# A linear-attention and two-MoE kernel: the first slot's transposes behind the last attention product, the last routing step earlier, slot 1's transposes inside layer 2, the next weights behind its rows

## The chip, the cores and the metric

The kernel runs on one core of a Trainium2 chip. The metric is the device time of one execution in microseconds (us), from the first to the last instruction of the core and what the program needs around it. A core has five engines with instruction queues of their own: TensorE (PE: matrix products and transposes; weight loads are listed as PEld), VectorE (DVE), ScalarE (ACT), GpSimd (POOL) and SyncE (SP, which here only issues DMAs). They meet through semaphores. POOL issues the indirect DMAs (gathers and scatters by row number), SP the plain ones.

## The reference

Three stages follow each other. The first is a linear attention with decay over 4 batches, 8 heads, 768 positions of 64 numbers in blocks of 64. Its output, 3072 rows of 512 numbers, goes through two mixtures of experts with 8 experts each, in which every row takes the one expert that its router prefers:

```python
for b in range(nb):                                   # attention, block by block
    intra = (qb @ kb.T * Dmask) @ vb
    inter = (qb * lam_pow) @ kv_state
    out[:, :, sl] = intra + inter
    kv_state = lam_block * kv_state + (kb * rev_pow).T @ vb
x = attn_out.transpose(0, 2, 1, 3).reshape(B * S, H * D)
...
logits = x @ w_gate + modality_bias[modality_id]      # first MoE
e_idx = np.argmax(logits, axis=1)                     # gate_w: softmax at e_idx
for e in range(E):
    h = np.maximum(x[mask] @ w1[e], 0.0)              # 512 -> 1024
    out[mask] = gate_w[mask, None] * (h @ w2[e])      # 1024 -> 512
...
do_compute = x @ w_skip > 0                           # second MoE: only these rows
y[mask] = gate_w[mask, None] * (h @ w2[e]);  out[do_compute] = xc + y
```

## The kernel before

**Attention.** 24 units (6 chunks of 128 positions times 4 batches) run through a pipeline written out by hand. In step i of the loop `for i in range(N + 1)`, PE makes unit i-1's product with the state (`stage_inter`), unit i's state update (`stage_kv`), unit i-1's product within the block (`stage_intra`; with the first it is the attention output, which ACT copies into `xr`), unit i+1's transposes and scores, and `stage_x(i - 2)`: four transposes of a finished `xr` into the bank `pmi`, from which ACT copies them to `xt` for the router. The routing of a chunk of four units is cut into `route_1` (router product from `xt`), `route_2` and `route_3` (choice of the expert, on DVE), `route_4` (ranks within the expert, two small products on PE, and the gate on DVE) and `route_5` (four indirect writes by POOL into a table in DRAM, `tab`, that lists each expert's rows). The last chunk's routing is done within the first slot of the MoE.

**Slots.** A MoE works through slots of 256 rows of one expert. A slot reads its list of rows (`load_ix`, SP), gathers the rows (`gather_x`, POOL, two halves of 128 rows), transposes them (`trans_x`: per half four transposes on PE, a cast `xth` by ACT, the remainder `xtl = x - xth` by DVE), and runs `layer1` and `layer2`. Every operand is split into a rounded high part and a low part, so each product is three matmuls (high x high, high x low, low x high). `layer1` is 8 steps f of 12 matmuls of 256 columns; after every second step ACT writes `hh` (relu) and DVE `hl` (its low part). `layer2` runs once for each half j of the rows: 8 steps of 3 matmuls of 512 columns, two steps for each quarter g of the weights `w2h[g]`, `w2l[g]`. Weights arrive in `raw1` and `raw2`; `split_w1` and `split_w2` cast the high part on ACT (L294, L300) and subtract on DVE (L295, L301).

**Order.** All instructions of an engine stay in the order in which the program calls them. In `layer1(kk, steps)` the entry `steps[f]` is called right behind the instructions of step f, so it decides what DVE, ACT and PE do between two steps. `table(which)` is a generator of three parts on DVE: the first ends with the first rows of all slots, which `load_ix` needs; the second says which expert comes next, which `ld_w1` and `ld_w2` need; the third says which slots are more than half full.

The first slot of the first MoE is `first1()`: it takes the largest expert on the rows counted so far, so its weights and rows are loaded during attention. In the last steps of attention its w1 is split in halves by the table `SPL`. `trans_x(0, 0, ...)` writes the attention's bank pair `psS`; here the second half's transposes carry a wait for DVE's `xtl` of the first half. The first slot of the second MoE is `first2()`, whose body `arm` is built the same way; in it `split_w2` and `layer2` take the quarters in the order 3, 2, 1, 0, and `ld_w1` there waits for the gathered rows (a dependency "the rows first"). The remaining slots are unrolled with runtime branches (`slots`, `slot`).

## Time and profile before

| | |
|---|---|
| median of 3 runs | 757.86 us (755.03 to 761.19) |
| the profiled execution | 751.07 us, its span 749.4 us |
| PE busy | 674.8 us, 90% of the span |
| DVE, ACT, POOL busy | 357.6, 266.6, 251.0 us |
| mean granted TensorE clock | 0.962 of full speed |

The span falls into attention (to about 137 us), the first MoE (to about 500 us) and the second (to the end). PE is busy throughout the middle of both MoEs, and its idle stretches lie at the seams: at the end of attention, in the first slot and at the first slot of the second MoE. A busy share says little of such a seam; the rows below show who waits for whom in these places. Times in them are microseconds from the start of the span; in brackets stands how long the engine was idle before, and what ended that.

### The profile page before, as it was taken

To read this page: it belongs to the slowest core of one execution; us is meant where nothing else is said; L and a number is where in the kernel's file an instruction comes from. 1 tells how busy PE (TensorE), PEld (TensorE's weight loads), DVE (VectorE), ACT (ScalarE), POOL (GpSimd) and SP (SyncE) were. 2 spreads that over 40 slices of the span, in tenths; PEclk is the share of its full clock that TensorE was granted. 3 is DMA by queue.
4 is the path that set the end of the run, shared out by engine and by line. 5 is a ranking of instruction groups with operands and counts; after the bars stand their busy time and mean duration, and the time that the engine had idled before them with its cause. 6 is when DMAs were issued, how large, how long until landed. Compare 5 with 4: busy or idle time off the path is not lost. (4 is left out here: it accounts for less than half of the span.)

```text
span 749.4 us, 18996 instructions
## 1 busy us (share of the span) xinstructions
PE 674.8 (90%) x7060; PEld 593.2 (79%) x7060; DVE 357.6 (48%) x873; ACT 266.6 (36%) x472; POOL 251.0 (33%) x306
## 2 busy tenths in 40 slices
PE   6878787769999999979999998877899999998994
PEld 5667666658889888778899887766799998897993
DVE  5455465481233025661331335646424566576850
ACT  2444242432222214642222225343013455546540
POOL 6445354343222224463122313461311221122231
PEclk9999899698999999989999999899899999999998
DMA  9757579219122212884111211450631766757600
GB/s 298 233 180 225 164 208 302 64 31 337 59 72 97 86 48 70 291 289 141 69 59 63 67 49 42 141 197 5 212 125 53 248 213 211 235 197 228 219 19 27
DMA packets 56568, 110.04 MB, mean 147 GB/s; under 512 B 18272, under 2 KB 18400, under 8 KB 56400
## 3 DMA queue, kind: packets, MB, share of 16 engines
q1 hardware_dynamic: 44432, 86.65, 35.6%
q0 software_dynamic: 9744, 20.47, 8.3%
q8 instruction: 76, 1.25, 0.7%
q10 hardware_dynamic: 2224, 0.93, 0.5%
q14 instruction: 92, 0.75, 0.4%
HBM read 84.08 MB, written 30.06 MB: 152 GB/s over the span
## 5 line engine op out<-in xcount | busy, mean ns | idle before, releaser
L716 PE MATMUL p<-xth,w1h 128*128 128x256 f32 x672 | 194.6, 290 | 10.1 <-DVE nm L151 4.5
L718 PE MATMUL p<-xth,w1l 128*128 128x256 f32 x672 | 189.2, 281 | 0.1
L717 PE MATMUL p<-xtl,w1h 128*128 128x256 f32 x672 | 189.2, 282 | 0.0
L724 DVE SCALAR_TENSOR_TENSOR hl<-p,hh 128x512 fp32r<-128x512 f32 x84 | 57.9, 691 | 190.2 <-ACT hh L723 190.2
L759 PE MATMUL p<-w2h,hl 128*128 128x512 f32 x360 | 143.3, 398 | 4.1 <-DVE hl L724 4.1
L716 PEld LDWEIGHTS p<-xth,w1h 128*128 128x128 f32 x672 | 128.8, 192 | 21.0 <-issue 12.9
L757 PE MATMUL p<-w2h,hh 128*128 128x512 f32 x360 | 143.6, 399 | 0.7 <-ACT hh L723 0.7
L758 PE MATMUL p<-w2l,hh 128*128 128x512 f32 x360 | 142.6, 396 | 1.3 <-DVE w2l L301 1.3
L161 POOL DMA_INDIRECT out_dram<-x2r,it x43 | 50.0, 1162 | 244.1 <-DVE x2r L768 114.9
L717 PEld LDWEIGHTS p<-xtl,w1h 128*128 128x128 f32 x672 | 129.2, 192 | 0.7
L718 PEld LDWEIGHTS p<-xth,w1l 128*128 128x128 f32 x672 | 128.8, 192 | 0.3 <-DVE w1l L625 0.3
L723 ACT ACTIVATE hh<-p 128x512 fp32r<-128x512 f32 x84 | 50.3, 598 | 195.4 <-PE p L718 187.8
L759 PEld LDWEIGHTS p<-w2h,hl 128*128 128x128 f32 x360 | 68.6, 190 | 18.8 <-DVE hl L724 4.8
L758 PEld LDWEIGHTS p<-w2l,hh 128*128 128x128 f32 x360 | 68.6, 190 | 16.7 <-DVE w2l L301 1.9
L757 PEld LDWEIGHTS p<-w2h,hh 128*128 128x128 f32 x360 | 68.6, 191 | 15.2 <-ACT hh L723 0.9
L165 POOL DMA_INDIRECT xg<-xs,it x54 | 62.0, 1147 | 40.9 <-issue 17.9
L161 POOL DMA_INDIRECT tab<-pk,rows x28 | 29.7, 1060 | 100.3 <-issue 85.6
L765 ACT ACTIVATE x2r<-p,it 128x512 f32<-128x512 f32 x26 | 17.9, 689 | 114.1 <-PE p L759 102.3
L300 ACT CAST w2h<-raw 128x1024 fp32r<-128x1024 f32 x48 | 48.8, 1049 | 25.7 <-issue 14.7
L301 DVE TENSOR_TENSOR w2l<-raw,w2h 128x1024 fp32r<-128x1024 f32 x45 | 52.3, 1220 | 9.1 <-ACT w2h L300 8.6
L295 DVE TENSOR_TENSOR w1l<-raw,w1h 128x1024 fp32r<-128x1024 f32 x38 | 51.7, 1419 | 2.4 <-ACT w1h L294 1.9
L473 POOL TENSOR_TENSOR qs<-kq,ltab 128x512 f32<-128x512 f32 x24 | 30.5, 1272 | 39.2 <-PE psO L534 28.7
(211 smaller groups left out, 867.3 us busy)
## 6 DMA issues: line engine op xcount, KB each, us to landing
raw<-in_w_dram SPq DMA_DIRECT2D x96, 512.0 KB, 6.8
kq<-in_qkv_dram SPq DMA_DIRECT2D x24, 512.0 KB, 5.5
xs<-x2r SPq DMA_DIRECT2D x28, 256.0 KB, 2.0
v<-in_qkv_dram SPq DMA_DIRECT2D x24, 256.0 KB, 4.1
xs<-xr SPq DMA_DIRECT2D x24, 256.0 KB, 4.6
xs<-xgm SPq DMA_DIRECT2D x7, 512.0 KB, 4.6
xg<-xs,it POOLq DMA_INDIRECT x54, 4.4
tab<-tini ACTq DMA_DIRECT2D x2, 416.0 KB, 7.5
```

Source lines behind the costliest of these rows:

```text
L161: nc.gpsimd.indirect_dma_start(out=dst, out_offset=bass.IndirectOffsetOnAxis(ap=idx, axis=0), in_=rows, in_offset=None, bounds_check=dst.s ...
L165: return nc.gpsimd.indirect_dma_start(out=rows, out_offset=None, in_=src, in_offset=bass.IndirectOffsetOnAxis(ap=idx, axis=0), bounds_chec ...
L295: (nc.gpsimd if c in pool else nc.vector).tensor_tensor(out=w1l[c], in0=raw1[:, c], in1=f32(w1h[c]), op=ALU.subtract)
L301: (nc.gpsimd if c in pool else nc.vector).tensor_tensor(out=w2l[c], in0=r, in1=f32(w2h[c]), op=ALU.subtract)
L716: nc.tensor.matmul(o, w1h[c][:, fs], xh[:, c, :], start=(c == 0), stop=False)
L717: nc.tensor.matmul(o, w1h[c][:, fs], xl[:, c, :], start=False, stop=False)
L718: nc.tensor.matmul(o, w1l[c][:, fs], xh[:, c, :], start=False, stop=(c == 3))
L723: nc.scalar.activation(out=a, in_=pt, func=AF.Relu)
L724: nc.vector.scalar_tensor_tensor(out=b, in0=pt, scalar=0.0, in1=f32(a), op0=ALU.max, op1=ALU.subtract)
L757: nc.tensor.matmul(p2[j], a, w2h[g][:, i], start=(n == 0), stop=False)
L758: nc.tensor.matmul(p2[j], a, w2l[g][:, i], start=False, stop=False)
L759: nc.tensor.matmul(p2[j], b, w2h[g][:, i], start=False, stop=(n == 7))
```

## The change

Five edits:

- `trans_x(0, 0, ...)` moves from ahead of the last `stage_intra` to behind the attention loop, and `stage_x(N - 1)`, until now step 0 of the first `layer1`, follows it there. The last quarter of w1 is split one attention step earlier (`SPL`).
- In the first `layer1` the last chunk's routing is called one step earlier (`route_1` in step 0 in place of 1, `mid` in 1 in place of 2, `late` in 3 in place of 4). The four splits of w2 are spread over steps 2, 3, 6 and 7, and the first part of the table moves from `late` to step 5.
- `layer2` gets a call `mid` behind its sixth step (18 of 24 matmuls). Slot 1's `trans_x` goes there, into the second half of slot 0's `layer2`; it stood ahead of that half. The conditional split of w1 (`split_next`) goes behind that half.
- `ld_w1` of the next expert in `first1` waits until both halves of slot 1's rows have landed (`behind`); on SP `ld_w2` and later DMAs are queued behind it.
- In `arm` the quarters of w2 are split and used in the order 0, 1, 2, 3.

```diff
-        SPL = {22: ((0, 0),), 23: ((0, 1), (0, 2)), 24: ((0, 3),)}
+        SPL = {22: ((0, 0),), 23: ((0, 1), (0, 2), (0, 3))}
...
-            if i == N:
-                trans_x(0, 0, [psS[:, j].rearrange("p (a t) -> p a t", t=P) for j in range(2)])
             if i:
                 stage_intra(i - 1)
...
         assert not sc
+        trans_x(0, 0, [psS[:, j].rearrange("p (a t) -> p a t", t=P) for j in range(2)])
+        stage_x(N - 1)
...
-    def layer2(which, kk, j, order=range(4)):
+    def layer2(which, kk, j, mid=None):
...
             nc.tensor.matmul(p2[j], b, w2h[g][:, i], start=False, stop=(n == 7))
+            if n == 5 and mid:
+                mid()
...
+    def behind(first, got):
+        for g in got:
+            tc.add_manual_dep(first.ins, g.ins.name, mybir.DependencyInfo(mybir.DependencyClass.Sync, mybir.DependencyReason.DATA),
+                              reason="the rows first")
...
                 route_5(NC - 1, t)
-            next(tb)
-            split_w2([0, 1])
+            split_w2([1])
...
-        layer1(0, {0: lambda: stage_x(NC * B - 1), 1: route_1, 2: mid, 4: late, 6: lambda: split_w2([2, 3])})
+        layer1(0, {0: route_1, 1: mid, 2: lambda: split_w2([0]), 3: late, 5: lambda: next(tb), 6: lambda: split_w2([2]),
+                   7: lambda: split_w2([3])})
...
+        got = gather_x(0, 1)
         e = reg(0, 2, 0, NE - 1)
-        ld_w1(e)
+        behind(ld_w1(e), got)
         ld_w2(e)
-        for i in range(1, 3):
-            gather_x(0, i)
+        gather_x(0, 2)
         fill()
         layer2(0, 0, 0)
-        trans_x(0, 1, ptr)
         fl = flag(0, 1)
+        layer2(0, 0, 1, lambda: trans_x(0, 1, ptr))
         split_next(0, 1, fl)
-        layer2(0, 0, 1)
...
-            split_w2([3, 2])
-            l1(0, {0: la, 1: lambda: (lg(), rk()), 3: lambda: rb(pcnt[1]), 5: lambda: (next(tb), split_w2([1, 0]))})
+            split_w2([0, 1])
+            l1(0, {0: la, 1: lambda: (lg(), rk()), 3: lambda: rb(pcnt[1]), 5: lambda: (next(tb), split_w2([2, 3]))})
...
-            layer2(1, 0, 0, (3, 2, 1, 0))
+            layer2(1, 0, 0)
```

The end of attention on PE. L534 is `stage_inter`, L545 `stage_intra` (`v` and the scores `P` into `psO`), L357 `stage_x`, L335 `trans_x` (`xg_157` and `xg_158` are the two halves of slot 0's rows); + and - are after and before.

```order
 L534 MATMUL psO<-s_2730,qs 64x64
+L545 MATMUL psO<-v,P 64x64 x16
+L357 MATMUL pmi<-ident,xr_189 128x128 x4
 L335 MATMUL psS<-ident,xg_157 128x128 x4
 L335 MATMUL psS<-ident,xg_158 128x128 x4
-L545 MATMUL psO<-v,P 64x64 x16
-L357 MATMUL pmi<-ident,xr_189 128x128 x4
```

The last product of attention and unit 22's transposes come ahead of slot 0's transposes.

DVE in the first `layer1`, between `route_3` (L133, the running counts `rs`) and `route_4` (L141, L143): L301 makes a low quarter of w2, L724 `hl`.

```order
 L133 TENSOR_TENSOR rs_123<-rs_123,oh 128x8 x4
-L724 SCALAR_TENSOR_TENSOR hl_2858<-p_2873,hh_2856 128x512
+L301 TENSOR_TENSOR w2l_153<-raw_140,w2h_149 128x1024
+L724 SCALAR_TENSOR_TENSOR hl_2863<-p_2878,hh_2861 128x512
 L141 COPY rs_123<-rs_123 128x8
 L143 TENSOR_TENSOR rk<-oh,pmi 128x32
```

The first quarter of w2 is now split ahead of `route_4` on DVE.

PE at slot 1's transposes (L335 into `ptr`, from `xg_159` and `xg_160`) within slot 0's `layer2` (L757 to L759; `w2h_149` to `w2h_152` are the quarters 0 to 3). Before:

```order
L759 MATMUL p_2875<-w2h_152,hl_2859 128x512
L335 MATMUL ptr_2871<-ident,xg_159 128x128 x4
L335 MATMUL ptr_2872<-ident,xg_160 128x128 x4
L757 MATMUL p_2876<-w2h_149,hh_2856 128x512
L758 MATMUL p_2876<-w2l_153,hh_2856 128x512
```

After:

```order
L759 MATMUL p_2881<-w2h_151,hl_2864 128x512
L335 MATMUL ptr_2876<-ident,xg_159 128x128 x4
L335 MATMUL ptr_2877<-ident,xg_160 128x128 x4
L757 MATMUL p_2881<-w2h_152,hh_2862 128x512
L758 MATMUL p_2881<-w2l_156,hh_2862 128x512
```

The 18 matmuls of the first three quarters of the second half now stand ahead of the transposes, the 6 of the last quarter behind them.

PE at the start of `layer2` in `arm`, the first slot of the second MoE (`hh1`, `hl1` are the second half of the hidden rows, `hh0`, `hl0` the first). Before:

```order
L718 MATMUL p10_2870<-xth0_167,w1l3_148 128x256
L757 MATMUL p20_2875<-w2h3_152,hh1_2857 128x512
L758 MATMUL p20_2875<-w2l3_156,hh1_2857 128x512
L759 MATMUL p20_2875<-w2h3_152,hl1_2859 128x512
L757 MATMUL p20_2875<-w2h3_152,hh1_2857 128x512
```

After:

```order
L718 MATMUL p10_2875<-xth0_167,w1l3_148 128x256
L757 MATMUL p20_2880<-w2h0_149,hh0_2861 128x512
L758 MATMUL p20_2880<-w2l0_153,hh0_2861 128x512
L759 MATMUL p20_2880<-w2h0_149,hl0_2863 128x512
L757 MATMUL p20_2880<-w2h0_149,hh0_2861 128x512
```

The quarter that needs the last written part of `hl` comes last in place of first.

## Rows read from the trace of the kernel before

**Rows 1.** Timeline of PE, end of attention (start us, us, engine, line, operation, count)

```profile
129.82 0.37 PE L545 MATMUL psO<-v,P 64*64 64x64 f32 x2
...
136.66 1.11 PE L335 MATMUL psS<-ident,xg 128*128 128x128 f32 x4 [1.83 <-DMA xg<-xs,it]
139.17 1.12 PE L335 MATMUL psS<-ident,xg 128*128 128x128 f32 x4 [1.40 <-DVE xtl L339]
140.22 1.14 PE L545 MATMUL psO<-v,P 64*64 64x64 f32 x32
...
142.10 0.58 PE L716 MATMUL p<-xth,w1h 128*128 128x256 f32 x1
```

**Rows 2.** Timeline of ACT, the splits of w1 in the last attention steps

```profile
129.47 1.14 ACT L624 CAST w1h<-raw 128x512 fp32r<-128x512 f32 x2
...
134.28 2.18 ACT L624 CAST w1h<-raw 128x512 fp32r<-128x512 f32 x4
```

**Rows 3.** Timeline of PE, first slot: layer 2 and slot 1's transposes

```profile
156.21 0.39 PE L757 MATMUL p<-w2h,hh 128*128 128x512 f32 x1
157.92 0.51 PE L758 MATMUL p<-w2l,hh 128*128 128x512 f32 x1 [1.33 <-DVE w2l L301]
...
163.34 0.39 PE L759 MATMUL p<-w2h,hl 128*128 128x512 f32 x1
168.09 2.28 PE L335 MATMUL ptr<-ident,xg 128*128 128x128 f32 x8 [4.37 <-DMA xg<-xs,it]
...
177.49 0.28 PE L716 MATMUL p<-xth,w1h 128*128 128x256 f32 x1
```

**Rows 4.** Timeline of POOL, first slot: the last routing's writes, slot 1's gather

```profile
153.47 0.98 POOL L161 DMA_INDIRECT tab<-pk,row  x1 [10.90 <-DVE t_n L181]
...
164.09 1.05 POOL L165 DMA_INDIRECT xg<-xs,it  x1 [5.37 <-DMA it<-tab]
```

**Rows 5.** Timeline of the SP queue, first slot: row lists and next weights

```profile
161.44 2.75 SPq L325 DMA_DIRECT2D it<-tab  x3
167.28 2.76 SPq L285 DMA_DIRECT2D raw<-in_w_dram  x4
```

**Rows 6.** Timeline of DVE, first slot: two of the four splits of w2

```profile
156.65 2.35 DVE L301 TENSOR_TENSOR w2l<-raw,w2h 128x1024 fp32r<-128x1024 f32 x2
```

**Rows 7.** Windows: span, PE PEld DVE ACT POOL busy (count), PEclk, DMA share, GB/s

```profile
167.00:168.00 1.00, 0.00 (x0) 0.00 (x0) 0.67 (x3) 0.00 (x0) 0.76 (x1) 0.62 0.73 168
174.00:175.00 1.00, 1.00 (x6) 0.81 (x5) 0.00 (x0) 0.00 (x0) 0.00 (x0) 0.97 1.04 324
180.00:320.00 140.00, 138.35 (x936) 122.55 (x934) 51.08 (x155) 47.67 (x83) 46.62 (x52) 1.00 0.35 118
545.00:675.00 130.00, 130.00 (x863) 118.63 (x861) 71.91 (x82) 56.38 (x72) 26.07 (x21) 1.00 0.55 181
```

**Rows 8.** Timeline of PE, first slot of the second MoE

```profile
506.50 0.36 PE L716 MATMUL p<-xth,w1h 128*128 128x256 f32 x1 [2.96 <-issue]
...
520.44 0.50 PE L757 MATMUL p<-w2h,hh 128*128 128x512 f32 x1 [0.69 <-ACT hh L723]
...
525.25 0.80 PE L759 MATMUL p<-w2h,hl 128*128 128x512 f32 x1 [4.08 <-DVE hl L724]
...
537.65 1.04 PE L335 MATMUL ptr<-ident,xg 128*128 128x128 f32 x8
...
540.10 0.38 PE L716 MATMUL p<-xth,w1h 128*128 128x256 f32 x1 [1.41 <-DVE xtl L339]
```

**Rows 9.** Timeline of DVE, first slot of the second MoE

```profile
522.23 2.36 DVE L301 TENSOR_TENSOR w2l<-raw,w2h 128x1024 fp32r<-128x1024 f32 x2
...
529.12 0.17 DVE L271 CAST ei<-t_w 128x24 int32<-128x24 f32 x1
```

**Rows 10.** Timeline of POOL there: the second gather of slot 1

```profile
529.48 1.02 POOL L165 DMA_INDIRECT xg<-xs,it  x1 [2.13 <-PE p L758]
```

**Rows 11.** Timeline of the SP queue there

```profile
533.06 2.11 SPq L285 DMA_DIRECT2D raw<-in_w_dram  x4
```

More of the change, by code (lines that the diff above doesn't have):

```diff
@@ L750, in layer1_half @@
             st_()
-    def layer2(which, kk, j, order=range(4)):
+    def layer2(which, kk, j, mid=None):
         js = slice(j * P, (j + 1) * P)
-        for n, c in enumerate(2 * g + i for g in order for i in range(2)):
+        for n, c in enumerate(range(8)):
             g, i = c // 2, c % 2
@@ L829, in arm @@
             gather_x(1, 2)
-            layer2(1, 0, 0, (3, 2, 1, 0))
+            layer2(1, 0, 0)
             next(tb)
             for j in js:
-                layer2(1, 0, j, (3, 2, 1, 0))
+                layer2(1, 0, j)
             trans_x(1, 1, ptr)
```

## The prediction

> **What bounds the kernel now.** I read the windows first. From 180 to 320 us PE is busy for 138.35 of 140 us, and from 545 to 675 us for all 130, at full clock [rows 7]. There a slot costs what its matmuls cost, and nothing in the change touches them. So the question is what the seams cost, and how much of it comes back. For these I read PE's timeline with the releaser of each idle stretch, and then, for the engine named, its own timeline.
>
> First seam, end of attention and first slot. PE runs out at 134.8 and waits for slot 0's rows until 136.66, then from 137.8 until 139.17 for DVE's `xtl` of the first half; only then come the last attention product (1.14) and the first `layer1` at 142.10 [rows 1]. Layer 2 begins at 156.21, waits 1.33 for a low quarter of w2, and its first half ends at 163.6. Then PE stands 4.37 us, until slot 1's rows land at 168.09 [rows 3]. That is the largest idle stretch here, and it costs twice: the clock falls during it (mean 0.62 of full in 167 to 168) and is back only in 174 to 175 [rows 7], so the transposes and the first matmuls of the second half run at the lower of the two levels, 1.2 in place of 2.4 GHz. Slot 1's `layer1` starts at 177.49 [rows 3].
>
> Second seam, first slot of the second MoE. Layer 2 could begin at 519.75; PE waits 0.69 for ACT's last `hh` and then 4.08 for DVE's last `hl`, until 525.25 [rows 8], because quarter 3 comes first and DVE makes two low quarters of w2 (522.23 to 524.59, [rows 9]) ahead of that `hl`. Slot 1's transposes follow at 537.65, its `layer1` at 540.10 [rows 8].
>
> **The change, first seam, step by step.**
>
> *The last product first.* It is free as soon as PE is (134.8), if the marker that ACT's queue gives it doesn't wait for the six casts ahead of it. It does not: the product of the unit before ran at 129.82 [rows 1] while ACT's two casts ran from 129.47 to 130.61 [rows 2]. So product to 136.0 and `stage_x(22)`'s four transposes (1.11 at this clock, like the four at 136.66 [rows 1]) to 137.1, in time that was idle; the rows are there since 136.66, and the first half's transposes end at 138.2. What is late next is ACT. Four casts took 2.18 [rows 2], so six end at 134.28 + 3.27 = 137.55; two copies and the cast `xth` follow at some 0.55 each, to 139.2. DVE's `xtl` (0.7) releases the second half's transposes at 139.9, against 139.17 before. From there to `layer1` before took 2.93 us [rows 1], with the product and four transposes behind; now only four transposes: the chain transposes 1.12, cast 0.6, `xtl` 0.7 gives 142.5. So `layer1` starts 0.4 **later**, and gets back 0.6 by four transposes less within it.
>
> *Routing one step earlier.* A step of `layer1` is worth (156.21 - 142.10)/8 = 1.76 us [rows 1, 3]. Against it stand the later start (0.4) and, on DVE, a low quarter of w2 that is now ahead of `route_4` (1.18, half of 2.35 [rows 6]). Net 0.2 earlier: the writes into the table start at 153.3 in place of 153.47, and what hangs on them by DMA alone keeps its distance [rows 4, 5]: lists 161.2, first gather 163.9, rows at 167.9, the second half some 1.1 later (its transposes ran without a gap behind the first's 1.1 [rows 3]), 169.0. PE itself now waits for the counts at `route_4`, some 0.6. So `layer1` takes its 14.1 again less the 0.6 and plus this 0.6, and layer 2 begins at 156.6 at the latest.
>
> *w2 spread out.* The quarters 0 and 1 are done before layer 2 begins, so the wait of 1.33 goes. The quarters 2 and 3 are behind the table's first part on DVE. From 153.2: quarter 1.18, `hl` 0.7, table 3.5 (before, it filled DVE from the writes' release to the splits at 156.65 [rows 4, 6]; I add some 0.3), quarter, `hl`, quarter: 161.6. Five matmuls of 0.24 (23 took 5.6 [rows 3]) stand behind that: first half done at 162.9, before 163.6.
>
> *Transposes inside layer 2.* The second half's 18 matmuls fill 4.3 us, to 167.2. PE waits 0.7 for the first half's rows (167.9), 0.6 for four transposes, 0.5 for the second half's rows (169.0), and after 0.6 more the last 6 matmuls (1.4) cover the cast and `xtl` (1.3). Slot 1 starts at 171.0. The idle rest is too broken to put the clock down by what the trace shows (its fall here came after 3.6 us of idle), so the slow stretch goes too. **171.0 against 177.49: 6.5 us.**
>
> *Weights behind the rows.* They start on SP at about 169.0 in place of 167.28 [rows 5]. Behind them stand `ld_w2`, the stores of slot 0's result and the next list, all of them some 10 us ahead of need; the window from 180 to 320 has 1.65 us of PE idle in all [rows 7], so the weights are not waited for in the next six slots. Cost nothing; if one load were awaited, 1.7.
>
> **Second seam.** DVE's queue is the same but for which quarter it makes. Layer 2 starts at 519.75 and 12 matmuls (2.8) on quarters 0 and 1 wait for nothing, to 522.55. Quarter 2 is ready at 522.23 + 1.18 = 523.4: a wait of about 0.7 behind its first matmul, then five more to 524.6. Quarter 3 is ready at 524.6 and the last `hl` at 525.2 [rows 8, 9], a wait of some 0.2. First half done at 526.2; second half, 24 matmuls, 5.6: 531.8, in place of 537.65. The slow clock after the wait goes as well.
>
> What is late next are slot 1's rows. The second gather is issued at 529.48 after 2.13 us that the profile puts down to PE [rows 10]; SP's weights, which wait for exactly these rows, start at 533.06 [rows 11]. The PE instruction named has nothing to do with those rows, so I let the gather stay where it is: rows at 533.0. Transposes of the first half fall into the wait, the second's take 0.5, cast and `xtl` 1.2: `layer1` at 534.8 against 540.10, **5.3 us**. Bounds: 4.6, if everything between transposes and `layer1` (540.10 - 537.65 = 2.45) follows 533.06; 6.0, if the gather moves up with PE (531.8 + 2.45 = 534.2). I take 5.3, nearer to the row of SP.
>
> On this gather a rule speaks too: DVE's last small operation ended at 529.29 [rows 9], 0.2 before it. The Trainium skill (SBUF — State Buffer, on who interferes with whom) says that a DMA issued by GpSimd needs a port to write its descriptors that some VectorE operations hold for their whole length. By that rule the gather would stay behind DVE's table, and the sum is the one taken; by PE's row it is 0.7 better. The first slot's gather went out at 164.09 [rows 4] with DVE in the same kind of table work, which the rule alone would not let me expect.
>
> **Sum.** 6.5 + 5.3 = 11.8 us. Both seams are followed by stretches in which PE has nothing to wait for, so they pass to the end. 751.07 - 11.8 = 739.3 for the profiled execution. The three runs lie higher than it (757.86 in the median); taken off that, **746.1 us**, 1.6% less. A measurement of this kernel tells a change from none at about 1%, 7.6 us.
>
> **Rivals.**
>
> 1. *ACT's queue holds the first slot up.* If the product waits for six casts (137.55 in place of 134.8), `layer1` starts some 2.2 later, and the clock, which needs a busy PE to rise, comes up later too. Rows land at 170.1, slot 1 starts at 173.1: 4.4 in place of 6.5. Should the broken waits at 167 to 169 also put the clock down, another 3.3 go (6.6 us at half speed, as from 167.4 to 174 [rows 7]). Against it stands the product at 129.82. Total 6.4 to 9.7: about 749.5.
>
> 2. *Rows earlier than I think*: PE doesn't wait at `route_4`, the writes move up by the whole step, the rows are there at 166.7 and PE never waits in layer 2 (slot 1 at 169.2, 8.3), and the gather of the second seam follows PE (6.0). Total 14.3: 743.6.
>
> 3. *Only one seam pays.* If slot 1's rows land 3 us later, or the reversal frees PE only to wait for rows that come at 537: 5.3 to 6.5, 752, no change that can be told.
>
> 4. *Slower: the code behind the branches.* PE waited 2.96 at 506.50 for nothing but its own queue [rows 8], ahead of the branch into `arm`. Ahead of slot 1's branch stood 24 matmuls that covered such a wait, now 6 and the transposes (2 us). Price: up to 2.96 at that place, about 748. It ends slower only if the moved code brings such waits to five slot entries or more that had none: five times 2.96 is 14.8, which gives 761. The 140 us with 1.65 idle speak against it, since some six entries lie in them. The Trainium skill (Runtime: NRT & Kernel Launch, on instruction fetch) says that a taken branch to code that is not loaded must wait for a fetch; the 2.96 looks like that, and the entries between 180 and 320 do not.
>
> **How the numbers follow.** Forecast 0.58 (10 to 13.5 us gained), rival 1 0.20, rival 2 0.10, rival 3 0.08, rival 4 0.04. Of rival 1 a good half is beyond 7.6 us. Faster by over 1%: 0.58 + 0.12 + 0.10 = 0.80; within 1%: 0.08 + 0.08 = 0.16; slower: 0.04. The range reaches from rival 2 less a spread of some 1.5 (the runs before lie within 3 of their median) to rival 1 plus 2: 742 to 751.5.
>
> **What would show it.** The last product ahead of the first L335 and `layer1` at 142 to 143; the table's last writes within 0.5 of 153.47; slot 1's transposes near 168 with waits under 1 us and its `layer1` near 171; no drop of PEclk between 160 and 180; in the second MoE no wait for `hl` above 1 us, slot 1's transposes waiting for the gather at the new place of 533, and as much PE time as before everywhere else. I am wrong if PE's product waits for the casts, if the rows come more than 2 us later, or if new idle time stands at slot entries.

## The result, and the profile after

The changed kernel takes **747.3 us** in the median of 4 executions (746.96 to 748.63), the kernel before beside it 757.94 (755.03 to 761.19). The ratio is **0.9884**, interval 0.9854 to 0.9915: 8.8 us less, 6.4 to 11.1; the medians differ by 10.6. On a second chip, measured later, both are some 5 us faster, 742.8 against 752.32, ratio 0.9861 (0.9824 to 0.9898). Forecast were 746.1 and a gain of 11.8.

The traced execution of the changed kernel took 747.03 us with a span of 745.2, that of the kernel before 751.07 and 749.4: between the traces lie 4.0 us only. So before a seam is read it must be known what differs between two executions of one kernel. I cut each span at six rows of PE: the last product of scores (L485), slot 0's first `layer1` matmul, slot 1's, the same two in the second MoE, and the second MoE's first matmul of a slot that runs in the short form (L735, `layer1_half`). The stretches are differences of the starts of those rows; the second trace of each kernel is from the experiments.

| stretch | before | before, 2nd | changed | changed, 2nd |
|---|---|---|---|---|
| A: to the last scores | 128.02 | 134.30 | 129.77 | 130.31 |
| B: to slot 0's layer1 | 14.08 | 17.24 | 14.28 | 14.67 |
| C: to slot 1's layer1, first seam | 35.39 | 33.75 | 29.92 | 29.80 |
| D: to the second MoE's layer1 | 329.01 | 326.94 | 328.64 | 326.85 |
| E: to slot 1's layer1, second seam | 33.60 | 34.07 | 29.80 | 32.45 |
| F: to the first short slot | 139.82 | 140.03 | 141.22 | 140.47 |
| G: to the end | 69.48 | 69.37 | 71.57 | 73.55 |

The trace of before from which the prediction was made is an early one: 6.3 us earlier than the second at the end of stretch A, 3.2 less in B. The change touches neither A nor D. C and E hold the seams; G, which nobody had named, is longer by more than 2 us.

First seam, PE's timeline of the changed kernel:

```profile
129.77 0.34 PE L485 MATMUL psS<-kq 64*64 64x64 f32 x6 [2.43 <-issue]
...
137.16 0.82 PE L545 MATMUL psO<-v,P 64*64 64x64 f32 x32 [1.49 <-ACTq L537]
...
139.01 1.12 PE L335 MATMUL psS<-ident,xg 128*128 128x128 f32 x4
141.53 1.12 PE L335 MATMUL psS<-ident,xg 128*128 128x128 f32 x4 [1.40 <-DVE xtl L339]
...
144.05 0.58 PE L716 MATMUL p<-xth,w1h 128*128 128x256 f32 x1 [0.55 <-DVE xtl L339]
...
162.58 0.50 PE L758 MATMUL p<-w2l,hh 128*128 128x512 f32 x1 [0.43 <-DVE w2l L301]
...
169.70 0.61 PE L335 MATMUL ptr<-ident,xg 128*128 128x128 f32 x4
171.10 0.66 PE L335 MATMUL ptr<-ident,xg 128*128 128x128 f32 x4 [0.79 <-DMA xg<-xs,it]
...
173.97 0.38 PE L716 MATMUL p<-xth,w1h 128*128 128x256 f32 x1 [0.82 <-ACTq L777]
```

They answer to [rows 1, 3]. The wait of 4.37 us for the rows has become 0.79, the transposes stand within layer 2, the wait of 1.33 for a quarter of w2 has become 0.43 here. New are 1.49 us ahead of the last product, put down to the marker in ACT's queue, and 0.82 at slot 1's entry. GpSimd's timeline, answering to [rows 4]:

```profile
156.33 1.70 POOL L161 DMA_INDIRECT tab<-pk,row  x1 [11.85 <-DVE pk L158]
...
166.14 1.16 POOL L165 DMA_INDIRECT xg<-xs,it  x1 [4.09 <-DMA it<-tab]
```

From this gather to slot 1's `layer1` it is 7.83 us (173.97 - 166.14); before it was 13.40.

Second seam, PE's timeline, and the gather on GpSimd's, answering to [rows 8, 10]:

```profile
502.61 0.37 PE L716 MATMUL p<-xth,w1h 128*128 128x256 f32 x1 [3.22 <-issue]
...
521.10 0.50 PE L758 MATMUL p<-w2l,hh 128*128 128x512 f32 x1 [0.96 <-DVE w2l L301]
...
529.37 0.60 PE L335 MATMUL ptr<-ident,xg 128*128 128x128 f32 x4
530.60 0.66 PE L335 MATMUL ptr<-ident,xg 128*128 128x128 f32 x4 [0.63 <-DMA xg<-xs,it]
532.41 0.38 PE L716 MATMUL p<-xth,w1h 128*128 128x256 f32 x1 [1.16 <-issue]
```
```profile
523.99 1.05 POOL L165 DMA_INDIRECT xg<-xs,it  x1 [7.14 <-DMA it<-tab]
527.16 1.02 POOL L165 DMA_INDIRECT xg<-xs,it  x1 [2.13 <-issue]
```

The 4.08 for the last `hl` are gone, 0.96 for a low quarter of w2 has come. PE waits 0.63 us for the rows.

The windows of the changed kernel (span, busy time and count of PE, PEld, DVE, ACT and POOL, granted clock, DMA share, GB/s) show that the clock no longer falls in the first seam (0.62 at this place before, [rows 7]), but falls behind the second and at the second MoE's first short slot:

```profile
167.00:168.00 1.00, 1.00 (x6) 0.83 (x5) 0.90 (x5) 0.00 (x0) 0.69 (x2) 1.00 0.07 9
...
171.00:172.00 1.00, 0.90 (x6) 0.86 (x7) 0.66 (x1) 0.21 (x1) 0.85 (x5) 1.00 0.63 217
...
535.00:536.00 1.00, 1.00 (x6) 1.00 (x6) 0.00 (x0) 0.00 (x0) 0.00 (x0) 0.50 0.99 397
...
675.00:676.00 1.00, 1.00 (x4) 0.75 (x3) 1.00 (x2) 0.00 (x0) 1.00 (x1) 0.50 0.95 344
```

Stretch G begins with the first of these rows in the changed kernel, and with the second in the kernel before:

```profile
673.63 0.77 PE L735 MATMUL p<-w1h,xth 128*128 128x512 f32 x1 [2.51 <-DVE w2l L301]
```
```profile
679.92 0.47 PE L735 MATMUL p<-w1h,xth 128*128 128x512 f32 x1 [2.01 <-DVE w2l L301]
```

The duration of the matmul tells the clock: 0.47 at the upper level, 0.77 when it has fallen. The DVE instruction named cannot be the releaser: in the trace of before the four splits of w2 run from 678.62 to 683.24, past the matmul.

### The profile page after: what moved, and what is told of

It is laid out like the page before. It is cut to its first block, busy times and chain, and to the rows that moved or that the text cites. A ratio compares the mean times of both kernels' runs of the same rounds, so it can differ in the third digit from the quotient of the medians.

```text
span 745.2 us, 19001 instructions
## 1 busy us (share of the span) xinstructions
PE 675.4 (91%) x7060; PEld 592.5 (80%) x7060; DVE 357.8 (48%) x873; ACT 267.9 (36%) x472; POOL 252.5 (34%) x306
## 4 chain that ended last, share of the span: by engine, by line
PE 64%; issue 5%; DVE 3%; DMA 2%; POOL 1%; ACT 0%; SPq 0%; DVEq 0%; ACTq 0%; POOLq 0%
PE p L716 10%; PE p L717 10%; PE p L718 10%; PE p L759 9%; PE p L758 9%; PE p L757 8%; PE ptr L335 2%; PE ptr L668 2%; DVE w1l L295 1%; PE pmi L673 1%; PE p L735 1%; PE p L737 1%; PE p L736 1%; DMA it<-tab 1%; PE pmi L678 1%
## 5 line engine op out<-in xcount | busy, mean ns | idle before, releaser
L716 PE MATMUL p<-xth,w1h 128*128 128x256 f32 x672 | 195.2, 291 | 11.4 <-DVE nm L151 4.5
L724 DVE SCALAR_TENSOR_TENSOR hl<-p,hh 128x512 fp32r<-128x512 f32 x84 | 57.9, 691 | 192.6 <-ACT hh L723 189.9
L757 PE MATMUL p<-w2h,hh 128*128 128x512 f32 x360 | 141.9, 394 | 0.0
L759 PE MATMUL p<-w2h,hl 128*128 128x512 f32 x360 | 141.8, 394 | 0.0
L757 PEld LDWEIGHTS p<-w2h,hh 128*128 128x128 f32 x360 | 67.6, 188 | 14.0
L759 PEld LDWEIGHTS p<-w2h,hl 128*128 128x128 f32 x360 | 67.7, 188 | 13.9 <-DVE hl L724 0.3
L295 DVE TENSOR_TENSOR w1l<-raw,w1h 128x1024 fp32r<-128x1024 f32 x38 | 56.8, 1553 | 4.3 <-ACT w1h L294 3.8
L301 DVE TENSOR_TENSOR w2l<-raw,w2h 128x1024 fp32r<-128x1024 f32 x45 | 52.4, 1219 | 8.6 <-ACT w2h L300 8.2
```

Of the source, the lines that this page charges most:

```text
L295: (nc.gpsimd if c in pool else nc.vector).tensor_tensor(out=w1l[c], in0=raw1[:, c], in1=f32(w1h[c]), op=ALU.subtract)
L301: (nc.gpsimd if c in pool else nc.vector).tensor_tensor(out=w2l[c], in0=r, in1=f32(w2h[c]), op=ALU.subtract)
L716: nc.tensor.matmul(o, w1h[c][:, fs], xh[:, c, :], start=(c == 0), stop=False)
L724: nc.vector.scalar_tensor_tensor(out=b, in0=pt, scalar=0.0, in1=f32(a), op0=ALU.max, op1=ALU.subtract)
L757: nc.tensor.matmul(p2[j], a, w2h[g][:, i], start=(n == 0), stop=False)
L759: nc.tensor.matmul(p2[j], b, w2h[g][:, i], start=False, stop=(n == 7))
```

## The experiments

Times of one block are from one chip, with the kernel before beside them.

**First block: which part brings what** (before 757.87).

*The second seam alone*, on the kernel before:

```
-            split_w2([3, 2])
-            l1(0, {... 5: lambda: (next(tb), split_w2([1, 0]))})
+            split_w2([0, 1])
+            l1(0, {... 5: lambda: (next(tb), split_w2([2, 3]))})
...
-            layer2(1, 0, 0, (3, 2, 1, 0))
+            layer2(1, 0, 0)
...
```

> The kernel before with one part of the change alone: in the first slot of the second MoE the quarters of w2 are split and used in the order 0, 1, 2, 3. Theory (the two seams add): the wait of 4.08 us for the last hl goes, slot 1's layer1 starts 5.3 us earlier counted from the entry of the arm (540.10 - 506.50 = 33.60 before, 28.3 here; bounds 4.6 and 6.0), and the time falls by 5.3 us, ratio 0.993. Rival A (only the first seam pays, because slot 1's rows land no earlier): 33.60 stays, no change, ratio 1.000 within 0.002. Rival B, from the trace of the changed kernel: the wait goes, but the short breaks for rows and branch put the clock down behind it, and 1.7 us of the 5.3 go again: 3.6 us, ratio 0.995.

Measured: 748.89, ratio 0.9897 (0.9853 to 0.9941). Stretch E fell to 28.42 us. In its timeline of PE:

```profile
510.24 0.36 PE L716 MATMUL p<-xth,w1h 128*128 128x256 f32 x1 [2.46 <-DVE itl L905]
...
527.38 0.50 PE L758 MATMUL p<-w2l,hh 128*128 128x512 f32 x1 [0.78 <-DVE w2l L301]
...
538.66 0.38 PE L716 MATMUL p<-xth,w1h 128*128 128x256 f32 x1 [1.17 <-issue]
```

Against 33.60, 34.07 and 33.70 in three traces of the old order that is 5.4 us, as the theory has it. The time fell by 7.8 us (4.5 to 11.1) by the ratio, more than this stretch shows, with the 5.4 in its interval. Rival A falls. The clock stayed up behind the seam (1.00 from 530 to 550), so rival B's loss doesn't always come. G is 69.80, as before.

*The first seam alone*, the complement: the changed kernel with the order 3, 2, 1, 0 put back in the second MoE. It was run last, on a chip where the kernel before takes 757.92.

```
...
-            split_w2([0, 1])
+            split_w2([3, 2])
...
-            layer2(1, 0, 0)
+            layer2(1, 0, 0, None, (3, 2, 1, 0))
...
```

> The changed kernel with the second MoE's first slot put back (quarters of w2 in the order 3, 2, 1, 0): the complement of the kernel that has the second seam alone. Theory (both seams pay): 29.9 us from layer1 to layer1 in the first MoE (33.75 to 35.39 in three traces of the old seam), 33.6 to 34.1 in the second; 4 to 5.5 us faster than the kernel before, ratio 0.993 to 0.995. Rival (only the second seam pays, since the kernel that has it alone came out at 0.9897, as low as both together): ratio 0.998 to 1.002, with the first seam's gain lost again further on.

Measured: 754.71, ratio 0.9976 (0.9949 to 1.0002). C is 29.87, E 33.70, as expected of the theory, but the time is not: 1.8 us less than before instead of 4 to 5.5. Most of the difference is found in G, 71.90 in place of 69.5:

```profile
540.58 0.38 PE L716 MATMUL p<-xth,w1h 128*128 128x256 f32 x1 [1.47 <-DVE xtl L339]
...
680.10 0.77 PE L735 MATMUL p<-w1h,xth 128*128 128x512 f32 x1 [2.58 <-DVE w2l L301]
```

So the rival is right in that part of the first seam's gain is lost further on.

*Slot 1's transposes between the halves of layer 2 again:*

```
         layer2(0, 0, 0)
+        trans_x(0, 1, ptr)
         fl = flag(0, 1)
-        layer2(0, 0, 1, lambda: trans_x(0, 1, ptr))
         split_next(0, 1, fl)
+        layer2(0, 0, 1)
```

> The changed kernel with slot 1's transposes of the first MoE (and the split behind them) put back between the two halves of layer 2. Theory (this move is what brings the first seam): PE stands idle again between the halves until the rows land, about 3.5 to 4.4 us, with the clock down for some us behind it; slot 1's layer1 starts 3.5 to 6.8 us later than in the changed kernel (29.92 us from layer1 to layer1 there, 33.4 to 36.7 here), time 750.8 to 754. Rival (the gain of the first seam comes from the routing that was moved up and from the weights that stand behind the rows): less than 1 us slower, 747 to 748.5.

Measured: 752.87, ratio 0.9935 (0.9896 to 0.9974), 5.6 us above the changed kernel by the medians, 3.9 by the ratios, whose intervals overlap. C is 36.70, 6.8 more: 1.5 of that lies ahead of slot 1's first gather (23.55 us behind `layer1` in place of 22.09, with `layer1` at the lower clock for its first 6 us), 5.3 behind it (13.15 in place of 7.83). Its timeline of PE and a window:

```profile
174.08 1.12 PE L335 MATMUL ptr<-ident,xg 128*128 128x128 f32 x4 [4.25 <-DMA xg<-xs,it]
175.49 1.11 PE L335 MATMUL ptr<-ident,xg 128*128 128x128 f32 x4 [0.29 <-DMA xg<-xs,it]
```
```profile
178.00:179.00 1.00, 1.00 (x4) 0.71 (x4) 0.00 (x0) 0.00 (x0) 0.84 (x2) 0.50 0.99 348
```

The wait is back, and with it the lower clock: theory.

*The front as before:* attention's end, the routing steps and w2's splits of the kernel before, everything else changed.

```
-        SPL = {22: ((0, 0),), 23: ((0, 1), (0, 2), (0, 3))}
+        SPL = {22: ((0, 0),), 23: ((0, 1), (0, 2)), 24: ((0, 3),)}
...
-        layer1(0, {0: route_1, 1: mid, 2: lambda: split_w2([0]), 3: late, 5: lambda: next(tb), ...
+        layer1(0, {0: lambda: stage_x(NC * B - 1), 1: route_1, 2: mid, 4: late, 6: lambda: split_w2([2, 3])})
```

> The changed kernel with the end of attention, the routing steps and the splits of w2 in the first slot as before (slot 0's transposes ahead of the last product, the last unit's four transposes at step 0 of layer1, routing one step later, w2 in pairs). Slot 1's transposes within layer 2, the weights behind the rows and the second seam stay changed. Theory (the prediction's sum: front and routing are worth 0.2 us of earlier rows and cover for a wait of 1.33): 0 to 1.5 us slower than the changed kernel, 747.3 to 748.8. Rival (the new front costs: its last product waits 1.49 us for ACT's queue, layer1 starts later): 1 to 2 us faster, 745.3 to 746.3. Second rival (the routing moved up brings most of the first seam): 3 us slower or more, from 750.3.

Measured: 750.65, ratio 0.9905 (0.9869 to 0.9941). C is 29.74 against 29.92, so it does not show a gain by the routing that was moved up. But the two ran slot 0's `layer1` at different clocks (1.00 here, 0.69 in the changed kernel, in the first 6 us), and the one trace of the new order at 1.00, of a kernel in the second block with one more edit, has C at 28.55; so up to 1.2 us for the routing is not ruled out. B is 15.60. Over all traces B is 14.08, 17.24, 14.87 and 15.60 with the old front and 14.28, 14.67, 14.21, 15.57, 15.54 and 14.78 with the new one: 0.6 less in the mean, in a spread of 3. By C the second rival falls, at least with its 3 us. The time settles little: the median of 750.65 is 3.4 above the changed kernel and would suit that rival, the ratio is 1.6 above and nearer to the theory, and the intervals overlap.

*The kernel before, unchanged:*

> The kernel before, unchanged, for a second trace of it and for what a measurement gives when nothing is changed. Theory (the traced execution of 751.07 us, some 7 under the median, was an outlier, and the median of the other executions is the kernel): ratio 1.000 within 0.004, and a trace with a span nearer to 756, its extra time in stretches that the change doesn't touch (attention and clock drops behind short waits). Rival (tracing itself makes the kernel faster by some 7 us, so that traced runs compare with traced runs only, and the change is worth 4 us): again 749 to 752 in the traced execution.

Measured: 758.99, ratio 0.9995 (0.9962 to 1.0027). The traced execution took 757.37. The rival falls; the traced 751.07 was low. Its span is 6.3 us longer: A has 6.3 more and B 3.2, C and D have 3.7 less. The 3.2 of B go with one wait on ACT, between its casts and the copy of slot 0's rows, at 147.24 in its timeline; the DMA view of 145 to 147 has one transfer on the queue of the instructions there (number, MB, share):

```profile
141.12 2.18 ACT L624 CAST w1h<-raw 128x512 fp32r<-128x512 f32 x4
147.24 0.58 ACT L338 CAST xth<-psS 128x512 fp32r<-128x512 f32 x1 [3.95 <-remote]
```
```profile
q8 instruction: 1, 0.02, 5.2%
```

ACT's inputs were there at 143.92, the end of the transposes, so a block of code that came late fits; it is not shown.

**Second block: the terms of the front** (before 752.32).

*The changed kernel, unchanged:*

> The changed kernel, unchanged, for a second trace. Theory (the two seams bring 5.3 each, and the rest of the difference between traces is the run): 29.9 us from slot 0's layer1 to slot 1's in the first MoE, 28.4 in the second (29.80 in the first trace, with the clock down at its entry), within 0.5; the time from the span's start to the last product of scores between 128 and 134, as in the other traces; median 747 to 749. Rival (the attention's end of the changed kernel is steadier or faster): the way from the last scores to layer1 stays at 14.3 within 0.3, where the kernel before had 14.08 and 17.24.

Measured: 742.8, ratio 0.9861 (0.9824 to 0.9898). C 29.80 as expected; E 32.45 in place of 28.4: at the entry of the second MoE's first slot PE stopped once more, 1.65 us, and ran `layer1` at the lower clock:

```profile
505.00:510.00 5.00, 5.00 (x28) 3.97 (x27) 0.88 (x1) 0.73 (x2) 0.35 (x3) 0.50 0.00 2
```

Layer 1 and its entry took 17.22 there, against 13.1 to 13.4 where the clock stays up and 14.40 in the first trace. From layer 2 on, E is the same in both, 15.40 and 15.23. B is 14.67 here and 14.21 to 15.57 in the six traces with the new front: not steady within 0.3 either.

*Weights not behind the rows:*

```
-        behind(ld_w1(e), got)
+        ld_w1(e)
```

> The changed kernel, but the next weights of the first MoE's first slot don't wait for slot 1's rows (they keep their place in the program behind the first gather). Theory (the weights behind the rows cost nothing and bring nothing): the same time as the changed kernel within 1 us, rows at the same place. Rival (they keep the queues free for the rows): the weights start some 2 us earlier, beside the gathered rows, whose second half then lands 0.5 to 1.5 us later, and slot 1 starts so much later: up to 1.5 us slower.

Measured: 743.78, ratio 0.9881 (0.9849 to 0.9912), 1.0 us above the changed kernel beside it, nothing that the times can tell. The weights started 2.63 us behind slot 1's first gather in place of 5.22 (172.41 - 167.19 in the second trace of the changed kernel), and from this gather to `layer1` it was 7.82, against 7.83 and 7.59. So the weights behind the rows cost nothing and bring nothing that shows. C is 31.19, 1.3 more than in the changed kernel, but that lies ahead of the gather (23.37 us behind `layer1`), where `layer1` started at the lower clock.

*A PSUM tile of its own for the second half of slot 0's rows:*

```
-        trans_x(0, 0, [psS[:, j].rearrange("p (a t) -> p a t", t=P) for j in range(2)])
+        trans_x(0, 0, [psS[:, 0].rearrange("p (a t) -> p a t", t=P), psT])
```

> The changed kernel, but the second half of slot 0's rows is transposed into a PSUM tile of its own (attention's tile of the transposed keys) in place of the other half of the tile that the first half uses. Theory (the wait of 1.40 us of the second half's transposes for DVE's xtl of the first half is only there because both stand in one tile): the two follow one another, layer1 starts 1.4 us earlier (14.27 us from the last scores to layer1, 12.9 here), what hangs on it moves along, and the kernel is 1.4 us faster, 745.9. Rival (the rows, or the casts in ACT's queue, are what the second half waits for): layer1 within 0.3 of its place, no change.

Measured: 739.81, ratio 0.984 (0.9804 to 0.9876); B 13.13, as expected, and C 28.55. The two transposes of slot 0's rows now follow one another, without the wait of 1.40:

```profile
138.18 0.66 PE L335 MATMUL psS<-ident,xg 128*128 128x128 f32 x4 [2.05 <-DMA xg<-xs,it]
139.14 0.66 PE L335 MATMUL psT<-ident,xg 128*128 128x128 f32 x4 [0.31 <-DMA xg<-xs,it]
```

*Four casts ahead of the marker in place of six:*

```
-        SPL = {22: ((0, 0),), 23: ((0, 1), (0, 2), (0, 3))}
+        SPL = {22: ((0, 0),), 23: ((0, 1), (0, 2)), 24: ((0, 3),)}
```

> The changed kernel, but the two casts of the last quarter of w1 stand behind the last product's marker in ACT's queue, as in the kernel before, so four casts and not six stand ahead of it. Theory (rival 1 of the prediction in part: ACT's marker goes out only when all but about three of the casts ahead of it are done, so the last product waits 1.49 us): the wait shrinks by two casts, 1.07 us, to 0.4 us; layer1 gains nothing from that if the last quarter's split then comes last, so 0 to 1 us faster, 746.3 to 747.3. Rival (the marker waits for something else): the wait stays at 1.5.

Measured: 744.51, ratio 0.9892 (0.985 to 0.9935). The last product didn't wait. But neither did it with six casts in the second trace of the changed kernel (product at 136.73, casts from 136.10 to 139.32), nor in five others; it waited 1.49, 1.83 and 2.07 in three. So the number of casts doesn't decide it, and both theories are left without a proof. B is 14.78 here, 14.67 with six casts and no wait, 14.28 with six and the wait: whatever it is, `layer1` doesn't hang on it.

**Third block: what the seams end on now** (before 752.36).

*The kernel with the second tile once more*, as a base:

> The changed kernel with the PSUM tile of its own for the second half of slot 0's rows, once more, as the base of the two kernels beside it. Theory (its gain of 1.4 us at the front and as much in the first slot is real): ratio to the kernel before within 0.981 to 0.987, 13.1 us from the last scores to layer1, 28.5 from layer1 to layer1. Rival (the first execution was a lucky one): ratio 0.986 to 0.989 like the changed kernel, 14 to 15 us and 29.9.

Measured: 742.37, ratio 0.9863 (0.9818 to 0.9909), between the two theories. This time the second half's rows came late:

```profile
140.43 1.12 PE L335 MATMUL psT<-ident,xg 128*128 128x128 f32 x4 [1.44 <-DMA xg<-xs,it]
```

and B is 15.47. The wait for the tile is removed, but where the rows of slot 0 come late, there is another of the same length behind it. Three measurements of this kernel (the third is the pad below) give 0.984, 0.9863 and 0.985, two of the changed one 0.9884 and 0.9861: perhaps 1.6 us better, not shown.

*Two low quarters of w2 on GpSimd:*

```
-            split_w2([1])
...
-        layer1(0, {0: route_1, 1: mid, 2: lambda: split_w2([0]), 3: late, ...
+        layer1(0, {0: lambda: (route_1(), split_w2([0, 1], (0, 1))), 1: mid, 3: late, ...
```

> As the base beside it, but in the first MoE's first slot the low quarters 0 and 1 of w2 are made by GpSimd ahead of its writes into the table, and not by DVE around the routing. Theory (the first seam ends on slot 1's rows, and these on the writes into the table, which one quarter of 1.2 us on DVE ahead of the ranks holds up): the writes start about 0.5 us earlier counted from layer1 (10.60 us in the base), slot 1's layer1 as much (28.0 in place of 28.5), and PE's wait for a low quarter of w2 (0.42) goes without moving the end: 0.5 us faster, no change that the times can tell. Rival A (the low quarters bound the slot): more than 1 us. Rival B (GpSimd beside DVE slows both, and the writes come later): 0.5 us slower or more.

Measured: 746.37, ratio 0.9896 (0.9845 to 0.9947), by the ratios 2.5 us above the base, with intervals that overlap: the times alone do not tell it from the base. The trace does, and shows rival B. GpSimd's timeline, then DVE's:

```profile
149.77 4.72 POOL L301 TENSOR_TENSOR w2l<-raw,w2h 128x1024 fp32r<-128x1024 f32 x2 [4.53 <-ACT w2h L300]
157.77 0.99 POOL L161 DMA_INDIRECT tab<-pk,row  x1 [3.29 <-DVE pk L158]
```
```profile
151.99 0.18 DVE L117 TENSOR_REDUCE m<-L 128x4 f32<-128x32 f32 x1
152.21 2.33 DVE L119 TENSOR_TENSOR d<-L,m 128x32 f32<-128x32 f32 x1
154.57 0.19 DVE L121 SCALAR_TENSOR_TENSOR sc<-d,pri 128x32 f32<-128x32 f32 x1
```

A subtraction of 32 columns that takes 0.19 elsewhere was held until GpSimd's second split was done (149.77 + 4.72 = 154.49). PE waited 1.99 us behind it for the chosen experts, and went on at the lower clock. The writes started 14.22 us behind `layer1`, in the base 12.39; the gather came 3.79 later than in the base, and C is 34.12 in place of 30.50, 3.62 more: slot 1 follows its gather.

*Eight small memsets on GpSimd ahead of the second MoE's first gather of slot 1:*

```
+            pad = hp.tile([P, 8], F32, name=f"pad{len(js)}")
+            for i in range(8):
+                nc.gpsimd.memset(pad[:, i:i + 1], 0.0)
             got = gather_x(1, 1)
```

> As the base beside it, but eight memsets of one column stand on GpSimd ahead of the second MoE's first gather of slot 1, in time in which GpSimd waits anyway. Theory (the second seam ends on slot 1's rows, and the pause of 2.13 us between their two gathers, equal in every trace whatever DVE and PE do, belongs to a place in GpSimd's own code): the pause moves off that place, the second gather goes out 1.8 us earlier, slot 1's rows land earlier, and layer1 starts up to 0.5 us earlier, when PE's own work ends it. Rival (the pause belongs to the pair of gathers, a wait or a queue): 2.13 us stay, nothing moves.

Measured: 741.64, ratio 0.985 (0.9804 to 0.9896), as its base. GpSimd's timeline:

```profile
514.85 0.36 POOL L829 MEMSET pad<- 128x1 f32 x8
521.91 1.04 POOL L165 DMA_INDIRECT xg<-xs,it  x1 [6.69 <-PE p L759]
525.08 1.02 POOL L165 DMA_INDIRECT xg<-xs,it  x1 [2.14 <-issue]
```

The pause stayed. Rival.

## Why the prediction came out as it did

**The two moves it rested on are shown.** The second seam: 5.4 us by stretch E, 5.3 predicted, in a kernel with this edit alone (the bound of 6.0 in the prediction comes to 5.9 by its own numbers, which changes nothing). Its steps held: waits of 0.7 and 0.2 forecast, 0.96 or 0.78 found, none for `hl`; the rows were awaited 0.63 us, and the gather stayed where it was, apart from the entry. The first seam: taking the transposes out of layer 2 again costs 5.3 us behind slot 1's gather, and with them there the clock stays at 1.00 up to slot 1 in all ten traces.

**The first seam's term was mis-sized.** The prediction had C at 171.0 - 142.5 = 28.5 against 35.39, 6.9 us, of which 0.4 was paid in B. Found were 29.92, 29.80 and 29.87; and the old seam gave 35.39, 33.75 and 34.84, so 0.7 of it was the one execution that was read. That leaves 4.8 in the mean. (The chain to `layer1` adds up to 139.9 + 1.12 + 0.6 + 0.7 = 142.3; the prediction carries 142.5.) The missing 1.4 of C lies in two steps: the gather came 22.1 us behind `layer1` where 163.9 - 142.5 = 21.4 was forecast, and the rest lies behind the gather.

The first is "routing one step earlier", and in it "`layer1` takes its 14.1 again". The prediction has the writes at 153.3 - 142.5 = 10.8 us behind `layer1`; they came 12.28, 12.01 and 11.84 behind it (before 11.37, 11.27 and 11.94), and layer 2 began 14.96, 14.91 and 14.73 behind it. What goes with this is the clock at which `layer1` starts. The windows of its first 6 us in the kernel before, the changed one, the one with a tile of its own, and the one without the weights behind the rows:

```profile
142.10:148.10 6.00, 5.89 (x67) 5.36 (x66) 1.99 (x3) 3.08 (x6) 0.47 (x2) 0.90 0.12 44
144.05:150.05 6.00, 6.00 (x58) 5.52 (x59) 0.00 (x0) 0.40 (x2) 0.44 (x1) 0.69 0.01 0
141.20:147.20 6.00, 6.00 (x73) 5.67 (x74) 0.97 (x3) 1.80 (x3) 1.98 (x3) 1.00 0.02 3
142.22:148.22 6.00, 6.00 (x50) 5.29 (x51) 0.00 (x0) 0.40 (x2) 0.48 (x2) 0.51 0.01 0
```

In the two traces at 1.00 the writes came 10.60 (new order) and 10.81 (old order) behind `layer1`; at 0.88 and 0.90 (old) 11.3 to 11.4; at 0.66 to 0.76, five of the new order and one of the old, 11.8 to 12.4; at 0.50 to 0.54 (new; the kernel with GpSimd's splits left aside) 13.0 to 13.3. At one clock the two orders lie 0.2 apart or less, where the prediction has one step less a low quarter of w2, 1.76 - 1.18 = 0.6. So the routing's move is worth less than reckoned, and the rest of the lateness goes with the clock, which the sum took as before; from these numbers I estimate about half for each. That the clock comes up later stood in rival 1 only. The old front starts `layer1` shortly behind the last product of attention, the new one behind transposes with waits between them; that this is why its clock is lower (0.66 in the mean of ten traces, 0.88 in the four of the old front) fits and is not shown. In the trace at full clock C is 28.55, the 28.5 of the prediction, but in part by luck: its gather comes 0.6 earlier than forecast, and the second step takes as much back.

The second step is slot 1's entry. From the gather to `layer1` the prediction has 171.0 - 163.9 = 7.1 us; it took 7.59 to 8.05. PE stands 0.82 us at this entry in all ten traces with the transposes inside layer 2, and not at all in the four with them ahead of the half. Rival 4 names this place; the sum has nothing for it.

**Both seams end on the gather.** In the ten traces with slot 1's transposes inside layer 2, its `layer1` starts 7.59 to 8.05 us behind its first gather in the first MoE, wherever the gather stands (20.8 to 26.4 us behind slot 0's `layer1`). In the eleven with the new order of quarters it is 8.35 to 8.66 in the second MoE. With the old seams it was 11.9 to 13.4 and 13.8 to 14.1. In the first MoE the way from the start of layer 2 to slot 1 varies more, 14.5 to 16.2, so the gather is the fixed point there. In the second that way is as steady (15.02 to 15.41) and cannot tell; there it is the rows that PE still awaits, 0.34 to 0.63 us in all eleven. A wait for a low quarter of w2 ends ahead of these, so it should cost nothing; that is argued from the order of the rows.

**The end of attention.** "It does not wait for the casts" failed in the first trace (1.49) and held in the second. That wait is one of the signs by which the prediction would call itself wrong; another, new idle time at a slot's entry, came with the 0.82 and in G. The forecast that `layer1` comes 0.4 later is lost in a spread of 3 us; in the mean it came 0.6 earlier. The 1.40 for `xtl` between the halves, which the prediction kept as part of the chain, is there only because both halves stand in one PSUM tile: with two tiles it was gone in all four traces, in one of them replaced by a wait for late rows.

**Weights behind the rows** cost nothing, as forecast.

**What was not named: stretch G.** The prediction lets both gains "pass to the end". They do not quite. G is 69.37 to 69.80 in the three traces without an edit of the first seam, 70.31 to 74.13 in the eleven with some or all of them, 72.2 in the mean: 2.7 us more. PE waits there 2.01 to 2.65 in the three and 2.31 to 3.50 in the eleven, and behind it the clock is at 1.00 in all three and under it in nine of eleven. At this row PE enters the short form of a slot, all its operands are long there, and no instruction ends the wait. That is the kind of rival 4, code behind a branch, at a fifth of the price it needed to make the kernel slower. But the short form alone does not bring it: the first MoE enters it twice (at about 300 and 450 us), with no wait above 0.05 in any of the fourteen traces. The edits of the first seam come with it; that they move the code, and that this is what lengthens the wait, is argued and not shown: the code of the short form is the same, 18996 instructions ran before and 19001 after. The Trainium skill (Runtime: NRT & Kernel Launch, on instruction fetch) says that a taken branch to code that isn't loaded waits for a fetch; no run here takes the branch away.

**The sum.** Worked out from the stretches: C 4.8, B 0.6, E 5.4, less 2.7 in G: 8.1. Two losses come with the clock. It falls at the entry of the second MoE's first slot in five of ten traces with both ends of the change (1.1 to 4.1 more in E), in none of the four others. And it falls behind the second seam in six of the eleven traces with the new order of quarters: F is 140.93 to 142.21 there and 139.14 to 140.47 in the other eight, where the prediction says that the slow clock goes as well. Spread over these traces that is an estimated 1.2 and 0.9 us, which leaves 6.0; the two spans of the changed kernel are 5.9 below the two of the kernel before in the mean. Measured were 8.8 (6.4 to 11.1) and 10.5 (7.7 to 13.2), so about 3 to 4.5 us of the measured gain are in no stretch that I can name; A alone ranges from 126.7 to 134.3. The forecast of 11.8 had 2.1 too much in C, nothing in G and nothing for the two falls of the clock; the 1.0 by which B came out better is lost in its spread. By the medians (10.6) the forecast came out, and that is in part luck: its terms, measured one by one, give 6 to 8. By the ratio (8.8) the time is one that rival 1 gives; its mechanism, the wait for the casts, was there in the first trace and not in the second, with the same `layer1`, but its later clock was in both. Rival 3 (one seam pays) is not borne out by its mechanism, since the rows came at both seams, with waits of 0.79 and 0.63; by the times it is nearer than its 0.08 said: alone, the first seam gives 1.8 us (none to 3.9), the second 7.8 (4.5 to 11.1), where the traces show 4.8 and 5.4.

## What to carry to other kernels

Work that waits for a transfer belongs inside the last stretch of matmuls that don't need it, so that the rest of them covers what follows the transfer: here that turned 4.4 us of idle into 0.8, and the clock's fall behind it went too. Read the granted clock at the start of a stretch of matmuls, before and after: here the first `layer1` began at 0.50 to 1.00, and the writes behind it moved by up to 2.7 us with it. Cut both spans at rows that the change cannot touch before comparing: two traces of one kernel differed by 6.3 us ahead of the change, more than either seam is worth. And look past the last edited line: here a stretch 500 us later was longer in every kernel with edits of the first seam.

## What the runs showed of the hardware

A DVE instruction with two operands in SBUF was held by GpSimd's subtraction for its whole length: 2.33 us in place of 0.19, ending with it. The evictions from PSUM beside it were not (`hl` at 151.16, 0.69). The Trainium skill (SBUF — State Buffer, on who interferes with whom) states just that: one of the two gets the shared ports for the whole instruction and the other is blocked, and the trace agrees. The other rule of that page, by which the prediction explained the late second gather, doesn't fit: the pair's first gather starts 3.17 to 3.19 us ahead of it in all fourteen traces, while DVE's last table operation ends 0.09 to 0.30 ahead. The pause goes with the two gathers; neither PE nor DVE nor eight instructions more ahead of it move it, and what it is stays open.

Whether a short idle stretch of PE puts the clock down is not told by its length: at the entry of the short slot it stayed up behind 2.65, 2.87 and 3.01 us and fell behind 2.31. The prediction's reading, that broken idle does not put it down, held at the first seam in ten traces of ten and at the second in five of eleven.
